# A chain of attention and two feed-forward layers on one core: the pooled values of two head pairs added up by TensorE in PSUM, and a new order of issue

## The chip, the cores and the metric

The kernel runs on one core of a Trainium2 chip. A core has TensorE (PE in the profile; PEld is its loading of weights), VectorE (DVE), ScalarE (ACT), GpSimd (POOL) and SyncE (SP), which here issues every DMA. The metric is the time of one execution on the device in microseconds (us); the profile's span is a little shorter, since it runs from the first to the last instruction.

## The reference

Attention over 4 batches of 8 heads, 576 positions, head size 64; then two feed-forward layers of 2304 tokens, width 512, hidden width 2048. What the change touches is the pooled part of the attention:

```
factor = 4
q_d = q.reshape(B, H, Sd, factor, D).mean(axis=3)      # Sd = 144
k_d = ...;  v_d = v.reshape(B, H, Sd, factor, D).mean(axis=3)
out_d = sm_attn(q_d, k_d, v_d)                         # softmax(q_d k_d^T / 8) v_d
out_up = np.repeat(out_d, factor, axis=2)
... out_local: each position attends to the 3 before and the 3 behind it ...
return out_up + out_local
```

Then `x = moe(x)` with `g = max(h,0) + log1p(exp(-|h|))`, and `moe2(x)` with `g = h * cos(h)`, where `h = x @ w_in` and the result is `g @ w_out`.

## The kernel before

The 32 heads are taken as 16 pairs, p00 to p33 (batch, pair of the batch). The first four, p00 to p03, make the first 512 tokens, from which the first layer starts. A pair goes through steps that the code names by letters. A writes the local scores to PSUM, B the pooled scores (Bm for the first four pairs, Bj inside A for the others). A2, A3, A4, A5, A6 are the local softmax on VectorE and ScalarE, B1, B2, B4 the pooled one. C and D turn the two sets of weights by TensorE (into tiles that ScalarE copies to aT and aTd). E multiplies: `pooled_values` the pooled weights with the pooled values, then 22 matmuls per head with the values themselves (vw, L1199). `up` and E1 add both and write the pair's columns of the tokens (raw0 to raw3 for the first four pairs, one tile each).

The pooled values are made like this before: a tile vd holds the pair's values as 3 blocks of 128 partitions, with the four rows r of a position side by side. `sum3` adds rows 0, 1 to rows 2, 3 (384 results per partition), `sum4` the two that are left (192 results) and writes the tile vs; both are VectorE instructions at L591. `pooled_values` then issues four matmuls: one per head with 128 partitions (L1162), one per head for what is left of the 144 positions (64 partitions, L1167). All are fp32; the profile shows an fp32 matmul as two records.

The first layer (L1 0 f in the code, L1392) needs raw0 to raw3 and the weights w1i, 16 units of 128 columns; six units (f = 0 to 5) are done in fp32, four matmuls each, into two PSUM halves h0 and h1 by turns. Weights come as 64-bit floats, in blocks of 1 MB, into two staging tiles stg0 and stg1, and are made to fp32 by ScalarE (L744, L760) and VectorE (L765, "join2"); a staging tile comes free with its join2. `allmax` (L629, L635) spreads a maximum over the partitions by a small matmul into h, and VectorE reduces it (red).

The order in which each engine issues is fixed before the kernel runs: a planner orders all steps by due times, to which a table MOVES of 739 numbers adds shifts. Each engine then works strictly in that order. Where the planner expects TensorE to stand idle early in the kernel it puts in a filler, a matmul of zeros (L2215, 128x512) whose result nobody reads; fillers are instructions like all others, and stand in the order.

Tiles come in rings: three qk tiles, two vd, three vw, two stg, four double PSUM banks (any0 to any3). A tile's next load waits until its last reader is done, and all loads stand in one order on SP.

Of the kernel before, what the change touches and what calls it, by code (L numbers as in the profile page):

```python
# [24 lines left out]
B, H, S, D = 4, 8, 576, 64  # L25
# [3 lines left out]
SD = S // 4  # L29
# [15 lines left out]
PV = 0  # L45
# [429 lines left out]
def pe(us):  # L475
    return {"pe": us}
# [27 lines left out]
def build(tc, qk, vw, vd, mask, w1i, w1o, w2i, w2o, out):  # L504
    nc = tc.nc
# [1797 lines left out]
```

## Time and profile before

| | |
|---|---|
| time, median of three runs | 828.73 us (827.4 to 828.96) |
| profiled execution: its time, its span | 827.2 us, 825.4 us |
| TensorE busy | 811.2 us, 98% of the span |
| VectorE busy | 736.4 us, 89% |
| ScalarE busy | 524.9 us, 64% |
| HBM read, written | 128.04 MB, 19.40 MB |

Busy time of TensorE includes the 64 fillers, which are no work. So a slice in which TensorE is nine tenths busy can still be one in which it waits; the fillers' own rows tell how much.

### The profile page before, as it was taken

What the parts mean: (1) busy time and instruction counts of PE and PEld (TensorE: products, weight loads), DVE (VectorE), ACT (ScalarE), POOL (GpSimd) and SP (SyncE); (2) the same over time, 40 slices, a digit from 0 to 9 for tenths busy, and PEclk for the clock granted to TensorE, in tenths of its full rate; (3) what the DMA queues carried; (4) which work ended last, traced back from release to release, by engine and by line L of the source; (5) the groups of instructions that cost most, each with busy time, mean ns of one, the idle gap of its engine ahead of it and who ended that gap; (6) DMA issues with size and microseconds to landing.
All of it is one profiled execution on the core that took longest, in us unless ns stands there. A gap on an engine that the chain in (4) does not pass through costs nothing.

```text
span 825.4 us, 17050 instructions
## 1 busy us (share of the span) xinstructions
PE 811.2 (98%) x6970; PEld 554.5 (67%) x6970; DVE 736.4 (89%) x1473; ACT 524.9 (64%) x877; POOL 1.8 (0%) x9
## 2 busy tenths in 40 slices
PE   8989999999999999999999999999999999999997
PEld 3644454555555544444447888888888888888886
DVE  7989989988695679999898999999999999999773
ACT  5887899554233359798997767665645555646420
POOL 0000000000000000000000000000000000000000
PEclk9999999999999999999999999999999999999999
DMA  9987421112200025775674532545666684689574
GB/s 356 348 311 259 162 97 34 41 53 94 80 17 2 1 104 176 233 228 186 235 275 160 216 135 91 178 154 207 231 227 218 222 287 153 251 266 335 183 215 177
DMA packets 49790, 148.54 MB, mean 180 GB/s; under 512 B 3888, under 2 KB 22960, under 8 KB 45616
## 3 DMA queue, kind: packets, MB, share of 16 engines
q1 hardware_dynamic: 49712, 147.46, 51.6%
q8 instruction: 54, 0.88, 0.4%
q14 instruction: 24, 0.20, 0.1%
HBM read 128.04 MB, written 19.40 MB: 179 GB/s over the span
## 4 chain that ended last, share of the span: by engine, by line
PE 79%; ACT 7%; DMA 6%; DVE 6%; issue 1%; POOL 0%; DVEq 0%; ACTq 0%; SPq 0%; POOLq 0%
PE h L1500 20%; PE any L1826 19%; PE any L1724 19%; PE h L1456 16%; DMA stg<-w1i 2%; DMA stg<-w2i 1%; PE any L1199 1%; DMA stg<-w1o 1%; DMA xt<-scr_out 1%; ACT w1i_t L787 1%; PE any L1095 1%; ACT tab L1658 1%; PE any L939 1%; ACT tab L1670 1%; DMA vd<-vd 1%
## 5 line engine op out<-in xcount | busy, mean ns | idle before, releaser
L1456 PE MATMUL h<-xt,w1i_t 128*128 128x512 f16 (+1 forms) x888 | 179.9, 356 | 0.3 <-DVE red L635 0.3
L1724 PE MATMUL any<-g,w1o_t 128*128 128x512 f16 (+1 forms) x792 | 161.6, 353 | 0.2 <-DVE g L599 0.2
L1456 PEld LDWEIGHTS <-w1i_t 128*128 128x128 f16 x888 | 86.0, 98 | 82.9 <-issue 2.9
L1724 PEld LDWEIGHTS <-w1o_t 128*128 128x128 f16 x888 | 85.5, 98 | 79.5 <-issue 2.0
L1500 PEld LDWEIGHTS <-ri 128*128 128x128 f16 x1194 | 116.7, 98 | 13.9 <-DMA ri<-scr_in 0.2
L1826 PEld LDWEIGHTS <-w1i_t 128*128 128x128 f16 x762 | 74.5, 98 | 11.3 <-issue 2.8
L1500 PE MATMUL h<-tx,ri 128*128 128x256 f16 x636 | 81.7, 273 | 0.0
L1826 PEld LDWEIGHTS <-w1o_t 128*128 128x128 f16 x750 | 73.3, 98 | 8.8 <-issue 0.3
L1500 PE MATMUL h<-xt,ri 128*128 128x256 f16 x558 | 74.5, 273 | 0.0
L1826 PE MATMUL any<-ro,w1i_t 128*128 128x256 f16 x489 | 73.0, 273 | 0.9 <-DVE g L1785 0.5
L609 ACT ACTIVATE w1o_t<-gf 128x512 f16<-128x512 f32 (+1 forms) x68 | 39.5, 587 | 52.4 <-DVE gf L591 34.2
L1651 ACT ACTIVATE tab<-h,i 128x512 f32<-128x512 f32 (+1 forms) x64 | 39.6, 631 | 50.7 <-PE h L1456 46.5
L1826 PE MATMUL any<-ro,w1o_t 128*128 128x256 f16 x435 | 66.8, 273 | 0.1
L591 DVE TENSOR_TENSOR hs<-h,hs 128x512 f32<-128x512 f32 (+1 forms) x96 | 56.9, 595 | 0.9 <-PE h L1500 0.4
L609 ACT ACTIVATE w1i_t<-gf 128x256 f16<-128x256 f32 (+2 forms) x82 | 39.8, 506 | 26.1 <-DVE gf L591 13.0
L591 DVE TENSOR_TENSOR gf<-gf 128x256 f32<-128x256 f32 (+2 forms) x120 | 55.1, 471 | 0.2
L1826 PE MATMUL any<-xt,w1o_t 128*128 128x256 f16 x315 | 48.0, 273 | 0.0
L591 DVE TENSOR_TENSOR w1i_t<-gf,w1i_t 128x256 f16<-128x256 f32 (+2 forms) x91 | 46.2, 523 | 0.5 <-ACT w1i_t L609 0.4
L599 DVE SCALAR_TENSOR_TENSOR g<-tab,sg,g 128x512 f16<-128x512 f32 (+1 forms) x64 | 43.2, 680 | 2.6 <-ACT g L603 1.8
L591 DVE TENSOR_TENSOR w1o_t<-gf,w1o_t 128x512 f16<-128x512 f32 (+1 forms) x69 | 43.2, 634 | 0.9 <-ACT w1o_t L609 0.7
L1826 PE MATMUL any<-xt,w1i_t 128*128 128x256 f16 x273 | 42.9, 273 | 1.0 <-ACT g L603 0.4
L1785 DVE SCALAR_TENSOR_TENSOR g<-any,ik,g 128x512 f32<-128x512 f32 (+1 forms) x35 | 23.8, 693 | 18.6 <-PE any L1826 18.5
(236 smaller groups left out, 1376.2 us busy)
## 6 DMA issues: line engine op xcount, KB each, us to landing
ri<-scr_in SPq DMA_DIRECT2D x31, 896.0 KB, 4.8
ro<-scr_out SPq DMA_DIRECT2D x41, 512.0 KB, 4.8
xt<-scr_out SPq DMA_DIRECT2D x29, 512.0 KB, 5.7
qk<-qk SPq DMA_DIRECT2D x16, 589.0 KB, 4.7
stg<-w1i SPq DMA_DIRECT2D x8, 1024.0 KB, 6.7
stg<-w1o SPq DMA_DIRECT2D x8, 1024.0 KB, 5.6
stg<-w2o SPq DMA_DIRECT2D x8, 1024.0 KB, 5.6
stg<-w2i SPq DMA_DIRECT2D x8, 1024.0 KB, 5.7
```

The costliest lines, as they stand in the source:

```text
L591: eng[e].tensor_tensor(out=out, in0=in0, in1=in1, op=op)
L599: nc.vector.scalar_tensor_tensor(out=out, in0=raw, scalar=s, in1=other, op0=ALU.mult, op1=op)
L609: nc.scalar.activation(out=out, in_=in_, func=AF.Copy)
L787: nc.scalar.activation(out=out().rearrange("p (m e) -> p m e", m=2), in_=self.floats(b), func=AF.Abs, accum_out=self.bd[:, b : b + 1],)
L939: nc.tensor.matmul(pa.t[64 * h : 64 * h + 64, j, 64 * g : 64 * g + 64], tk.t[64 * j : 64 * j + 64, 0, q0 + 3 : q0 + 67], tk.t[64 * j : 64 ...
L1095: nc.tensor.transpose(pc.t[:, k, 128 * o : 128 * o + 128], sm.t[:, g, :, :].rearrange("p j k -> p (j k)"), ident)
L1456: nc.tensor.matmul(h.t[:, 0:n], l, r, start=(i == 0), stop=(i == 11))
L1500: nc.tensor.matmul(h.t[:, a : a + m], l, r, start=(i == 0), stop=(i == n - 1))
L1651: act(n, 1, True), lambda: nc.scalar.activation(out=x(), in_=h.t[:, 0:n], func=AF.Softplus, scale=col(o.i1, f)),
L1724: nc.tensor.matmul(a.t[:, i, 0:n], l, r, start=(first and j == 0), stop=(last and j == 2))
L1785: dve(256 * m, False, 1), lambda: nc.vector.scalar_tensor_tensor(out=o.t[:, 0 : 256 * m], in0=view(k), scalar=T[t].ik, in1=x.t[:, 0 : 256 ...
L1826: nc.tensor.matmul(a.t[:, z, 256 * c : 256 * c + 256], l, r, start=(b == 0 and x == 0), stop=(b == NB - 1 and x == 2),)
```

## The change

Where a pair's number is below PV (2 now, 0 before, so p00 and p01), sum3 and sum4 are not issued. `pooled_values` multiplies the pooled weights with each of the four rows of vd instead and lets the four products add up in the same PSUM region: 16 matmuls for the pair in place of 4. The planner's cost of step E for such a pair is set to 3.4 us. The table MOVES is another one, of 798 numbers. Lines behind L85 stand 14 lower in the new file.

```
-PV = 0
+PV = 2
...
-    "L1 0 0 ln#1": -314.5, "L1 0 1 exp#1": 70, "L1 0 1 mm#1": 963, "L1 0 10 G#1": 1002.5, "L1 0 10 abs#1": 29.5,
...
+    "tsum#12": 980.5, "tsum#13": 833, "tsum#15": 852, "tsum#17": 814.9, "tsum#3": 770, "tsum#6": 726, "tsum#7": 728.5,
...
             def pooled_values():
-                for j in range(2):
-                    o = slice(64 * j, 64 * j + 64)
-                    nc.tensor.matmul(
-                        po.t[o, 1 - quads, u0 : u0 + SD], vs.t[:, j, :], aTd.t[:, SD * j : SD * j + SD], start=True, stop=False
-                    )
-                for j in range(2):
-                    o, w = slice(64 * j, 64 * j + 64), left + 16 - 16 * j
-                    nc.tensor.matmul(
-                        po.t[o, 1 - quads, u0 : u0 + SD], vs.t[o, 2, :], aTd.t[o, w : w + SD], start=False, stop=True
-                    )
+                vals = [tv.t[:, :, r, :] for r in range(4)] if i < PV else [vs.t]
+                for z in (False, True):
+                    for n, v in enumerate(vals):
+                        for j in range(2):
+                            o, w = slice(64 * j, 64 * j + 64), left + 16 - 16 * j
+                            l, r = (v[o, 2, :], aTd.t[o, w : w + SD]) if z else (v[:, j, :], aTd.t[:, SD * j : SD * j + SD])
+                            nc.tensor.matmul(
+                                po.t[o, 1 - quads, u0 : u0 + SD], l, r, start=(not z and n == 0),
+                                stop=(z and n == len(vals) - 1),
+                            )
...
-            outs_of.append(aop(pe(3.5 if i < PV else ...
+            outs_of.append(aop(pe(3.4 if i < PV else ...
```

On VectorE, in the first 20 us, the order before was (vd1 and vs1 are p01's; qt, qd are sums of queries and keys; rs the row sums of a softmax; sm and ed its weights; w1i_t the join2 of a weight block):

```order
L591 TENSOR_TENSOR ed0_128<-ed0_128,rs_0_235 128x432
L591 TENSOR_TENSOR qd0_120<-qt0_119 128x288
L591 TENSOR_TENSOR vd1_115<-vd1_115 128x3x128
L978 TENSOR_REDUCE rs_1_236<-sm1_126 128x10
L591 TENSOR_TENSOR vs1_123<-vd1_115 128x192
L981 TENSOR_SCALAR rs_1_236<-rs_1_236 128x13
L965 TENSOR_REDUCE nm_2_233<-any0_87 128x10
L984 RECIPROCAL rs_1_236<-rs_1_236 128x13
L1046 TENSOR_REDUCE nd_2_241<-any1_88 128x3
L591 TENSOR_TENSOR sm1_126<-sm1_126,rs_1_236 128x640
L591 TENSOR_TENSOR ed1_129<-ed1_129,rs_1_236 128x432
L765 SCALAR_TENSOR_TENSOR w1i_t_164<-w1i_t_164,stg1_110 128x1024
```

At the same place, from ed of p00 to the join2 of the second block, it is now:

```order
L605 TENSOR_TENSOR ed0_128<-ed0_128,rs_0_235 128x432
L992 TENSOR_REDUCE rs_1_236<-sm1_126 128x10
L605 TENSOR_TENSOR qt0_119<-qk2_113 128x576
L979 TENSOR_REDUCE nm_2_233<-any0_87 128x10
L605 TENSOR_TENSOR qd0_120<-qt0_119 128x288
L995 TENSOR_SCALAR rs_1_236<-rs_1_236 128x13
L779 SCALAR_TENSOR_TENSOR w1i_t_164<-w1i_t_164,stg0_109 128x1024
L998 RECIPROCAL rs_1_236<-rs_1_236 128x13
L1060 TENSOR_REDUCE nd_2_241<-any3_96 128x3
L605 TENSOR_TENSOR sm1_126<-sm1_126,rs_1_236 128x640
L605 TENSOR_TENSOR ed1_129<-ed1_129,rs_1_236 128x432
L779 SCALAR_TENSOR_TENSOR w1i_t_164<-w1i_t_164,stg1_110 128x1024
```

The two sums of p01 are gone, and the join2 of the first weight block, which stood behind p00's raw0 before, has come ahead of p01's last softmax steps; the sum of p02's queries has moved down to here.

On TensorE step E of p00 (aTd0 and aT0 are the turned weights, zero is a filler) was this before:

```order
L1162 MATMUL any2_92<-aTd0_132,vs0_122 64x144 x2
L1167 MATMUL any2_92<-aTd0_132,vs0_122 64x144 x2
L1199 MATMUL any2_92<-aT0_130,vw0_116 64x58 x16
L1199 MATMUL any2_92<-aT0_130,vw0_116 64x48
L1199 MATMUL any2_92<-aT0_130,vw0_116 64x10
```

And now:

```order
L1180 MATMUL any2_92<-aTd0_132,vd0_114 64x144 x16
L1213 MATMUL any2_92<-aT0_130,vw0_116 64x58 x16
L1213 MATMUL any2_92<-aT0_130,vw0_116 64x48
L1213 MATMUL any2_92<-aT0_130,vw0_116 64x10
L1213 MATMUL any2_92<-aT0_130,vw0_116 64x48
```

Four matmuls on vs have become sixteen on vd, and E reads the tile that the load wrote. Ahead of E of p03, the last of the first four, stand 64 fillers now, where 58 did, and two matmuls of the first layer, where three did; behind it no filler is left, where 6 were.

Further on TensorE, where the first layer's fp32 units run and the tokens' maximum (am0) is spread, the order was, from the end of one unit to the step E of p10 (aTd0, vs1):

```order
L1392 MATMUL h0_627<-raw3_169,w1i_t_164 128x512
L629 LDWEIGHTS am0_243
L629 MATMUL h1_628<-ident_s_74,am0_243 128x128
L1392 MATMUL h1_628<-raw0_166,w1i_t_164 128x512
L1392 MATMUL h1_628<-raw1_167,w1i_t_164 128x512
L1392 MATMUL h1_628<-raw2_168,w1i_t_164 128x512
L1392 MATMUL h1_628<-raw3_169,w1i_t_164 128x512
L1162 MATMUL any2_92<-aTd0_132,vs1_123 64x144 x2
```

It is now, up to the next unit:

```order
L1406 MATMUL h1_691<-raw3_169,w1i_t_164 128x512
L643 LDWEIGHTS am0_243
L643 MATMUL h0_690<-ident_s_74,am0_243 128x128
L1180 MATMUL any0_87<-aTd0_132,vs2_124 64x144 x4
L1213 MATMUL any0_87<-aT0_130,vw1_117 64x58 x14
L1213 MATMUL any0_87<-aT0_130,vw1_117 64x42
L1213 MATMUL any0_87<-aT0_130,vw1_117 64x16
L1213 MATMUL any0_87<-aT0_130,vw1_117 64x42
```

Step E of p10 now stands between the spread of am0 and the next unit that writes the same half of PSUM; before, that unit followed the spread at once.

## Rows read from the trace of the kernel before

**Rows 1.** The page: busy time of each engine, share, instructions.

```profile
PE 811.2 (98%) x6970; PEld 554.5 (67%) x6970; DVE 736.4 (89%) x1473; ACT 524.9 (64%) x877; POOL 1.8 (0%) x9
```

**Rows 2.** Stretches: length, busy us of PE, PEld, DVE, ACT, POOL, clock, DMA.

```profile
0.00:44.57 44.57, 41.25 (x616) 24.11 (x617) 37.95 (x81) 32.11 (x86) 1.77 (x9) 1.00 0.92 352
44.57:69.04 24.47, 20.92 (x113) 9.38 (x110) 22.96 (x50) 21.39 (x38) 0.00 (x0) 1.00 0.78 274
69.04:140.00 70.96, 70.03 (x571) 35.11 (x571) 65.86 (x127) 63.86 (x121) 0.00 (x0) 1.00 0.38 132
140.00:760.00 620.00, 618.87 (x5135) 433.06 (x5134) 568.97 (x1121) 388.32 (x593) 0.00 (x0) 1.00 0.49 167
760.00:825.43 65.43, 60.09 (x544) 52.82 (x541) 40.67 (x101) 19.18 (x42) 0.00 (x0) 1.00 0.61 199
```

**Rows 3.** Line L2215, the fillers: ns shortest/median/longest, first and last start.

```profile
L2215 PE MATMUL any<-zero x56: 376/379/634, 2.1 to 68.7; 128*128 128x512 f16 x56
L2215 PE MATMUL h<-zero x8: 379/379/390, 29.0 to 36.8; 128*128 128x512 f16 x8
```

**Rows 4.** Timeline of PE: start, us, line, tiles, records [idle before, releaser].

```profile
2.06 4.02 PE L2215 MATMUL any<-zero 128*128 128x512 f16 x9 [2.06 <-POOL zero L2204]
...
20.08 0.47 PE L1162 MATMUL any<-aTd,vs 128*64 128x144 f32 x4
20.47 0.46 PE L1167 MATMUL any<-aTd,vs 64*64 64x144 f32 x4
20.77 1.48 PE L1199 MATMUL any<-aT,vw 64*64 64x58 f32 x44
22.18 1.25 PE L2215 MATMUL any<-zero 128*128 128x512 f16 x5
...
29.88 0.71 PE L1095 MATMUL any<-ident,sm 128*128 128x128 f32 x5
...
47.75 2.84 PE L1392 MATMUL h<-raw,w1i_t 128*128 128x512 f32 x6 [1.19 <-DVE raw L1223]
...
56.65 0.22 PE L629 MATMUL h<-ident_s,am 128*128 128x128 bf16 x1 [0.34 <-DVE g L1413]
57.59 3.70 PE L1392 MATMUL h<-raw,w1i_t 128*128 128x512 f32 x8 [0.73 <-DVE red L635]
...
66.67 0.22 PE L629 MATMUL h<-ident_s,bd_w1i 128*128 128x128 bf16 x1 [0.26 <-DVE g L1413]
67.65 0.38 PE L629 MATMUL h<-ident_s,bd_w1i 128*128 128x128 bf16 x4 [0.77 <-DVE red L635]
...
69.04 0.33 PE L933 MATMUL any<-mask_sb,ident_b 64*64 64x320 bf16 x4
```

**Rows 5.** Line L1095: weight loads of the turns, ns shortest/median/longest.

```profile
L1095 PEld LDWEIGHTS any<-ident,sm x80: 137/140/145, 15.3 to 286.5; 128*128 128x128 f32 x80
```

**Rows 6.** Timeline of DVE about the sums of p00 and p01.

```profile
5.63 0.56 DVE L591 TENSOR_TENSOR vd<-vd 128x384 f32<-128x384 f32 x1
6.23 0.36 DVE L591 TENSOR_TENSOR vs<-vd 128x192 f32<-128x192 f32 x1
7.47 0.61 DVE L1046 TENSOR_REDUCE nd<-any 128x3 f32<-128x432 f32 x1 [0.89 <-PE any L1040]
...
16.01 0.57 DVE L591 TENSOR_TENSOR vd<-vd 128x384 f32<-128x384 f32 x1
16.48 0.83 DVE L978 TENSOR_REDUCE rs<-sm 128x10 f32<-128x640 f32 x1
17.20 0.37 DVE L591 TENSOR_TENSOR vs<-vd 128x192 f32<-128x192 f32 x1
```

**Rows 7.** Waits of PE behind 69 us: waiting, releaser, us in total, times, longest.

```profile
PE any L1116 <- ACT ed L1063: 0.6, 1, 0.6
PE h L629 <- ACT stg L1997: 0.5, 1, 0.5
```

**Rows 8.** DMA issues of the values: count, KB each, median us to landing.

```profile
vd<-vd SPq DMA_DIRECT2D x8, 384.0 KB, 5.3
```

More of the change, by code (lines that the diff above doesn't have):

```diff
@@ L1206, in pair @@
             raws += [("x2g", 14 + c // 2)] if b == 2 else []
-            outs_of.append(aop(pe(3.5 if i < PV else 1.38 if small else 1.48 if quads else 2.11), Em, [tv if i < PV else vs, aTd, tw, (aT, 0), (aT, 1)], [po, *outs, *raws], [po, up, aT], nm + "E"))
+            outs_of.append(aop(pe(3.4 if i < PV else 1.38 if small else 1.48 if quads else 2.11), Em, [tv if i < PV else vs, aTd, tw, (aT, 0), (aT, 1)], [po, *outs, *raws], [po, up, aT], nm + "E"))
             if small:
```

296 rows, old and new, of the table MOVES are left out of this document.

## The prediction

> **What bounds the kernel now.** I read the busy shares first [rows 1]: TensorE is busy 98% of the span, every other engine less. Work that is added to TensorE therefore costs its length, unless it takes the place of time in which TensorE does nothing useful, and the stretches [rows 2] tell where that is. From 140 to 760 us TensorE idles 1.1 of 620 us, behind that 5.3 (the last results' way out is most of it). From 0 to 44.57 it idles 3.3, of which 2.06 are the start, from 44.57 to 69.04 3.55, from 69.04 to 140 0.9. The granted clock is 1.00 in all of these, so no term below is one of the clock. Fillers come on top: 64 of them [rows 3], the first nine in 4.02 us, later ones five in some 1.2 [rows 4], all before 69.04. So whatever can be won lies in the first 69 us: there TensorE runs in a row what stands in its order, fillers with it, and its real stops are few. Up to 44.57, the end of E of p03, they sum to 1.26 behind the start; between there and 69.04 the timeline shows one for raw3 (1.19 us) and four in the pattern "a small spread into h, then a wait for VectorE's reduction of it, or for the unit's result that frees h" (0.34, 0.73, 0.26, 0.77) [rows 4].
>
> **The sums that leave VectorE.** Each pair loses two instructions: 0.56 and 0.36 us for p00, 0.57 and 0.37 for p01 [rows 6]. Those of p00 ran while VectorE had nothing else: behind them it still waited 0.89 us for TensorE. They are worth nothing. Those of p01 ran in a full row; successive starts are 0.47 and about 0.27 apart, since neighbours overlap, so VectorE gets 0.74 us there. The new order spends it at once: the first block's join2 comes ahead of p01's last softmax steps, and p01's D is not earlier for it.
>
> **The products that come to TensorE.** Twelve more fp32 matmuls per pair, 24 records, issued by heads in twos that run side by side: 12 steps. The trace has no chain of 16, so I bound a step. Above: the two twos of L1162 take 0.39 us for two steps (20.08 to 20.47), 0.20 a step [rows 4], with the load of the second set of weights in the open. Below: an fp32 record of 512 columns takes (3.70 - 0.59) / 7 = 0.44 us in the unit at 57.59, so 144 columns stream 0.125 us. In long rows of one kind the loads hide: the 22 steps of L1199 take (1.48 - 0.22) / 21 = 0.06 us each at 58 columns, against 0.05 by the same stream, and the five 128-column turns at 29.88 follow each other at (0.71 - 0.27) / 4 = 0.11 us though each load takes 0.14 [rows 4, 5]. Sixteen alike are nearer to these, so I take the lower end: 1.5 us a pair, **3.0 us** in all; with 0.20 it is 4.7. Nothing excuses this time from TensorE's row: it is work, and neither end is below nothing, since no record gets shorter.
> A rule speaks against the change here. The Trainium skill, "TensorE: Matmul & The Clock Gate", section "The mechanism", says that loads of weights overlap with matmuls in flight only when the row group differs, and these sixteen use the same rows. By that rule a step would cost load and stream, 0.13 + 0.125 us, 3.1 us a pair and 6.1 in all in place of 3.0. The turns at 29.88, all 128 rows each time, contradict it here [rows 4, 5]; it stays as a rival below.
>
> **Fillers.** 64 before and after, but eight stand at the start, where nine did; a filler there takes 0.45, later 0.22 to 0.24: -0.2 us. Before E of p03 there are now 64, where 58 were, and one product of the first layer less (0.93). So E of p03 ends later: 44.57 + 3.0 + 1.3 - 0.9 - 0.2 = 47.8. Six fillers fewer stand behind it.
>
> **Stops up to E of p03.** E of p00 waits as before for ScalarE, whose order there still has the first step of the second weight block between two copies of aTd. C of p00 and A of p03 have 0.2 to 0.7 us to wait for. I take +0.1 against the 1.26 of before.
>
> **Stops from there to 69 us.** raw3 stopped TensorE because E of p03 was early and VectorE, in order, came to raw3 late (47.1). Now E ends at 47.8, and VectorE, which at raw3 has two joins more behind it (3.5 us), but not the sums of p00 and p01 nor one pair's sums of queries and keys (2.5; about +1.0 us), comes there at 48 to 49, while TensorE has two products (1.9 us) that don't need it. -1.2. The spread of am0 now has p10's E (1.47 us from its first matmul to the next unit) between it and the next unit of its half, which covers a wait of 0.73; the weights' spreads stand among products of the second matrix, which need no h. -2.1, of which I give back 0.2 for results (g) that may be late. What is late next is VectorE: in this stretch it was busy 23.0 of 24.5 us [rows 2]. Sum -3.1.
>
> **Behind 69 us.** Of the 0.9 idle, 0.6 is D of p11 waiting for ScalarE's ed [rows 7]; a further unit of 2.6 us stands ahead of it now: -0.5. In 140 to 760 the longest stop, 0.5 (with 0.2 behind it) is a spread of weight maxima waiting for ScalarE [rows 7]; in the new order these spreads stand some 30 matmuls of 0.22 us later: -0.7. The last 65 us are ordered anew with as many matmuls and the same last four results; I count 0, with 1.2 us either way.
> The values' tile is now read by E, not by the sums, so the two vd tiles come free later: p02's load goes out behind E of p00 (about 25.7, 6.8 before), and behind it on SP stand p11's queries, p03's vw and the fifth weight block. VectorE needs it at about 29 us, and the load takes 5.3 us in the median [rows 8], but with other loads queued ahead of it; by then the queue is short, so I count nothing for it. If that cover is gone, it is the third rival.
>
> **Sum.** Against the profiled execution, 827.2 us (span 825.4 and 1.8 around it): +3.0 - 0.2 + 0.1 - 3.1 - 0.5 - 0.7 = -1.4, so 825.8. The profiled execution lies 1.5 below the median of the runs shown, 828.73; carried over to that, 827.3 us. The bounds are +1.7 (products at the upper end), 1.2 either way (the tail), and -0.5 to +1 (stops that I gave or kept): own range 825.3 to 829.5. A measurement of this kernel can tell about 0.2%, 1.7 us, from no change.
>
> **Rivals.**
> 1. All stops vanish. If the new order fits as well as it is drawn, the 3.55, 0.9 and 1.1 of idle go whole and of the first 1.26 too: 827.2 + 2.8 - 6.8 = 823.2, 824.7 in the median's terms. For it: nearly all stops lie where the order was redrawn. Against it: VectorE is 94% busy from 44 to 69 us and can't be much earlier. Chance 0.20.
> 2. The change doesn't do what it says: VectorE's 0.74 us buys nothing, stops come back elsewhere, and TensorE pays for its products: 827.2 + 2.8 = 830.0, 831.5. For it: half of what leaves VectorE was hidden. Against: the stops of rows 4 have named causes that the order takes away. Chance 0.08.
> 3. Slower by the values' tile. Place: VectorE's sum of p02, which waits, in order, for a load that goes out only behind E of p00; p03's load hangs on that sum in turn. If the loads take the full 5.3 us, VectorE stands 2 us at each, and p03's softmax, C, E and raw3 with it: 825.8 + 3.9 = 829.7, 831.2. It decides from the point where each of the two waits passes 1.5 us. Against it: TensorE is itself late by then, which takes up the first microsecond. Chance 0.11.
> 4. The loads of the sixteen in the open. A step of 0.255 us, as two records one behind the other with a load between, gives 3.1 us more: 825.8 + 3.1 = 828.9, 830.4 in the median's terms. For it: the two twos of L1162 with 0.20 a step. Against it: the turns with 0.11. Chance 0.05. The rule of the skill named above says just this.
>
> **How the numbers follow.** My forecast has 0.50; 0.23 of it lies below 827.07 (faster by over 0.2%), 0.27 within 0.2%. Rival 1 is faster. Rivals 2 and 3 are slower, of rival 4 half. The remaining 0.06 is spread over lesser mixtures within 0.2%. Faster 0.43, same 0.36, slower 0.21. The range takes in half of rival 1 and most of rival 3: 824.0 to 831.3.
>
> **What would show it.** The new L1180 groups of 16: about 2.2 us from the first to the following L1213 (3.0 would be the upper bound, 3.7 rival 4). E of p03 should end at about 48 us. TensorE should reach the scores of p11 (the row that stood at 69.04) at 68 to 69.5, with less than 0.7 us of stops between; if stops on raw3 or on red stand there as before, the term -3.1 is wrong, and with it the sign. VectorE waiting for vd at p02's or p03's sum shows rival 3. A TensorE that idles more than 1 us from 140 to 760, or more than 6 behind that, would make the last terms wrong.

## The result: slower by one per cent

The changed kernel takes 836.11 us (median of four executions, 834.89 to 838.96) against 828.16 (827.4 to 828.96) for the kernel before, measured beside it: a ratio of 1.0102, with a 95% interval of 1.0078 to 1.0126. The forecast was 827.3, the range ended at 831.3. The profiled execution took 835.9 us, with a span of 834.1, and its span is 8.7 us longer than that of before.

### The profile after

The page of the changed kernel, busy time of each engine, to be held against [rows 1]:

```profile
PE 814.1 (98%) x7018; PEld 557.5 (67%) x7018; DVE 737.0 (88%) x1475; ACT 524.4 (63%) x875; POOL 1.8 (0%) x9
```

TensorE is busy 2.9 us longer; VectorE and ScalarE are within 0.6 us of where they were. So 5.8 of the 8.7 us are time in which TensorE does nothing. The stretches say where; they end at the same steps as those of [rows 2] (the end of E of p03, the scores of p11, 140, 760, the end). Columns: length, then busy us and records of PE, PEld, DVE, ACT, POOL, the granted clock, DMA.

```profile
0.00:51.42 51.42, 44.01 (x668) 27.15 (x668) 39.84 (x80) 34.32 (x84) 1.77 (x9) 1.00 0.86 323
51.42:72.22 20.80, 19.55 (x104) 8.86 (x101) 18.70 (x41) 18.23 (x39) 0.00 (x0) 1.00 0.86 313
72.22:140.00 67.78, 64.99 (x498) 31.80 (x498) 59.01 (x118) 56.27 (x110) 0.00 (x0) 1.00 0.37 126
140.00:760.00 620.00, 616.31 (x5127) 428.64 (x5127) 569.13 (x1122) 389.23 (x596) 0.00 (x0) 1.00 0.48 162
760.00:834.05 74.05, 69.20 (x628) 61.00 (x625) 50.30 (x118) 26.40 (x52) 0.00 (x0) 1.00 0.68 221
```

Length less busy time of PE, before and after: 3.3 and 7.4 up to the end of E of p03, 3.6 and 1.3 from there to the scores of p11, 0.9 and 2.8 from there to 140, 1.1 and 3.7 from 140 to 760, 5.3 and 4.9 behind. The stops between E of p03 and the scores of p11 did go, as the prediction said. New ones came ahead of that stretch and behind it. The scores of p11 begin at 72.22 in place of 69.04, 3.2 us late, and 5.5 us more are lost behind them (4.0 of them idle time of TensorE, 1.5 longer busy time), where the prediction had put nothing but small gains.

The timeline of PE shows what was foreseen (start, us, line, tiles, records, and in brackets the idle time before and what ended it):

```profile
22.32 2.33 PE L1180 MATMUL any<-aTd,vd 128*64 128x144 f32 x32
24.48 1.48 PE L1213 MATMUL any<-aT,vw 64*64 64x58 f32 x44
...
40.90 0.74 PE L1109 MATMUL any<-ident,sm 128*128 128x128 f32 x5 [2.23 <-DVE sm L605]
...
50.01 1.48 PE L1213 MATMUL any<-aT,vw 64*64 64x58 f32 x44
51.42 2.03 PE L1406 MATMUL h<-raw,w1i_t 128*128 128x512 f32 x4
53.90 1.98 PE L1406 MATMUL h<-raw,w1i_t 128*128 128x512 f32 x4 [0.44 <-DVE raw L1237]
...
63.53 0.22 PE L643 MATMUL h<-ident_s,am 128*128 128x128 bf16 x1 [0.17 <-DVE g L1427]
...
65.16 7.13 PE L1406 MATMUL h<-raw,w1i_t 128*128 128x512 f32 x16
72.22 0.33 PE L947 MATMUL any<-mask_sb,ident_b 64*64 64x320 bf16 x4
```

The 32 records of p00's pooled values take 24.48 - 22.32 = 2.16 us, where 0.69 stood [rows 4]. The stop at raw3 is 0.44 us in place of 1.19, that at the spread of x's maxima 0.17 in place of 0.34, and the four units at 65.16 run through. But C of p03 stops TensorE for 2.23 us at 38.67, and what it waits for is VectorE. VectorE's timeline ahead of that:

```profile
31.75 0.56 DVE L605 TENSOR_TENSOR vd<-vd 128x384 f32<-128x384 f32 x1 [1.90 <-DMA vd<-vd]
...
38.73 0.56 DVE L605 TENSOR_TENSOR vd<-vd 128x384 f32<-128x384 f32 x1 [0.96 <-DMA vd<-vd]
...
45.30 0.56 DVE L605 TENSOR_TENSOR vd<-vd 128x384 f32<-128x384 f32 x1 [1.90 <-DMA vd<-vd]
```

These are the sums over the values of p02, p03 and p10, each waiting for its load: the third rival of the prediction. Behind the scores of p11 the stops are spread; the longest four in the timeline of PE:

```profile
92.45 0.22 PE L643 MATMUL h<-ident_s,bd_w1o 128*128 128x128 bf16 x1 [2.06 <-DVE g L1427]
...
142.16 0.59 PE L1130 MATMUL any<-ident,ed 128*128 128x128 f32 x3 [0.62 <-DVE s_w1i L602]
...
180.26 0.76 PE L1109 MATMUL any<-ident,sm 128*128 128x128 f32 x5 [0.73 <-DVE sm L605]
...
241.29 0.47 PE L1188 MATMUL any<-aTd,vs 64*64 64x144 f32 x8 [0.71 <-ACT aT L623]
```

Two explanations offer themselves. HOLD: the tiles of p00's and p01's values are held until E, so later values load late, VectorE falls behind in the front and everything pays for that. ORDER: the order that was fitted anew, on all engines and for the whole kernel, is itself the worse one.

### The profile page after: what moved, and what is told of

Read it like the earlier page. It is cut to its first block, busy times and chain, and to the rows that moved or that the text cites. A ratio compares the mean times of both kernels' runs of the same rounds, so it can differ in the third digit from the quotient of the medians.

```text
span 834.1 us, 17153 instructions
## 1 busy us (share of the span) xinstructions
PE 814.1 (98%) x7018; PEld 557.5 (67%) x7018; DVE 737.0 (88%) x1475; ACT 524.4 (63%) x875; POOL 1.8 (0%) x9
## 4 chain that ended last, share of the span: by engine, by line
PE 65%; DVE 14%; DMA 9%; ACT 9%; issue 2%; SPq 1%; POOL 0%; DVEq 0%; POOLq 0%; ACTq 0%
PE h L1514 18%; PE any L1840 18%; PE any L1738 14%; PE h L1470 10%; DMA vd<-vd 3%; DMA stg<-w1o 2%; DMA stg<-w1i 2%; DMA stg<-w2o 1%; DVE sm L605 1%; DMA scr_out<-dec 1%; ACT ed L1077 1%; DMA stg<-w2i 1%; PE any L1213 1%; DVE hs L605 1%; DVE gf L605 1%
## 5 line engine op out<-in xcount | busy, mean ns | idle before, releaser
L1738 PEld LDWEIGHTS <-w1o_t 128*128 128x128 f16 x888 | 85.4, 98 | 78.9 <-issue 2.0
L1514 PEld LDWEIGHTS <-ri 128*128 128x128 f16 x1086 | 106.2, 98 | 12.6
L1840 PE MATMUL any<-ro,w1i_t 128*128 128x256 f16 x543 | 80.7, 273 | 0.4 <-ACT g L617 0.4
L1840 PEld LDWEIGHTS <-w1o_t 128*128 128x128 f16 x732 | 71.5, 98 | 9.4 <-issue 1.1
L1514 PE MATMUL h<-tx,ri 128*128 128x256 f16 x582 | 74.5, 273 | 0.0
L1514 PE MATMUL h<-xt,ri 128*128 128x256 f16 x504 | 67.1, 273 | 0.0
L1840 PE MATMUL any<-ro,w1o_t 128*128 128x256 f16 x417 | 63.7, 273 | 0.2 <-DVE g L1799 0.2
L623 ACT ACTIVATE w1o_t<-gf 128x512 f16<-128x512 f32 (+1 forms) x64 | 37.3, 590 | 39.0 <-DVE gf L605 30.9
L605 DVE TENSOR_TENSOR w1i_t<-gf,w1i_t 128x256 f16<-128x256 f32 (+2 forms) x93 | 47.8, 531 | 0.0
L1514 PEld LDWEIGHTS <-xt 128*128 128x128 f16 x450 | 44.0, 98 | 5.3 <-issue 0.3
```

The source lines that it names most:

```text
L605: eng[e].tensor_tensor(out=out, in0=in0, in1=in1, op=op)
L623: nc.scalar.activation(out=out, in_=in_, func=AF.Copy)
L1514: nc.tensor.matmul(h.t[:, a : a + m], l, r, start=(i == 0), stop=(i == n - 1))
L1738: nc.tensor.matmul(a.t[:, i, 0:n], l, r, start=(first and j == 0), stop=(last and j == 2))
L1840: nc.tensor.matmul(a.t[:, z, 256 * c : 256 * c + 256], l, r, start=(b == 0 and x == 0), stop=(b == NB - 1 and x == 2),)
```

## Experiments

All times are medians of 4 to 12 executions; the ratio is to the kernel before, run on the same chip beside it.

| run | us | ratio, 95% interval |
|---|---|---|
| vd4 | 834.12 | 1.0070, 1.0055 to 1.0086 |
| vd4_early | 834.85 | 1.0081, 1.0063 to 1.0099 |
| b_vd4 | 828.40 | 1.0003, 0.9990 to 1.0016 |
| b_own | 828.54 | 1.0013, 1.0001 to 1.0026 |
| h_own_p11 | 834.73 | 1.0087, 1.0068 to 1.0106 |
| h_after_p11 | 832.76 | 1.0070, 1.0044 to 1.0095 |
| h_own_p30 | 835.84 | 1.0101, 1.0080 to 1.0122 |
| h_after_p30 | 838.48 | 1.0128, 1.0102 to 1.0153 |
| eased | 836.94 | 1.0120, 1.0081 to 1.0158 |
| b_eased | 829.78 | 1.0026, 1.0012 to 1.0040 |
| vd4_light | 833.04 | 1.0053, 1.0026 to 1.0079 |
| own_light | 828.73 | 1.0014, 1.0002 to 1.0027 |
| order_alone | 836.72 | 1.0108, 1.0087 to 1.0130 |
| own_again | 828.90 | 1.0011, 0.9996 to 1.0027 |

### The tiles: vd4, vd4_early, b_vd4

The order of issue is planned as it was, and only then the first eight pairs' values are handed out to four tiles in place of two; the two new ones lie in the space of x's fourth tile.

```diff
+VDX, VDP = 4, 8
...
 ops, all4 = P.order(), list(BANK.tiles)
+for c in range(VDX - NVD):
+    VD.tiles.append(xt[3][:, 2 * c : 2 * c + 2].rearrange("p c (a r d) -> p (c a) r d", r=4, d=64))
...
+for m, v in enumerate(sorted(use, key=lambda v: use[v][0])):
+    v.i = min(range(VDX if m < VDP else NVD), key=lambda k: over[k])
+    assert over[v.i] < use[v][0]
+    over[v.i] = use[v][-1]
```

vd4 does this to the changed kernel, b_vd4 to the kernel before. vd4_early besides puts two loads forward in SyncE's row:

```diff
+MOVED = [('p02 vd#1', 'p02 vw#1'), ('p03 vd#1', 'p10 qk#1')]
```

> The changed kernel, order of issue on every engine untouched, but the first eight pairs' values have four tiles vd in place of two (two views of x's fourth tile, which nothing writes before the third batch entry). The load of p02's values then no longer waits for E of p00, and p03's not for the sums of p02. Theory HOLD (the loss of some 8 us is the tiles held until E, through VectorE's waits of 1.9, 0.96, 1.9 and 0.2 us for these loads): most of those 5.0 us comes back, and the stop of TensorE at C of p03 (2.2 us) with it: 831 to 833 us, ratio to the kernel before 1.003 to 1.006. Theory ORDER (the order fitted anew asks for things later or earlier than they are there, whatever the tiles): SyncE issues these loads behind other transfers and VectorE waits for other things instead: 834.5 to 836.5, ratio 1.008 to 1.010.

> As the run with four tiles vd, and the loads of the values of p02 and p03 moved forward in SyncE's row: p02's ahead of the load of its windows, p03's ahead of p10's queries, as early as the kernel before has them. Theory HOLD: VectorE's waits for values are gone to under 0.3 us in the first 40 us, and the time is at most that of four tiles alone, 830 to 833. Theory ORDER: what was wanted early now takes bandwidth from weights and queries, and VectorE waits for those: no gain over four tiles alone (within 0.5 us), or a loss of up to 1 us.

> The kernel before, order untouched, with the four tiles vd for the first eight pairs: the control for the runs with four tiles. SyncE there waited 9.4 us for the sums vs and 6.8 for a load vd before it could load values; VectorE never waited for values. HOLD and ORDER agree: the tiles are not short there, so 827.5 to 829, ratio 0.998 to 1.001.

VectorE's waits for loads in vd4, behind 27 us:

```profile
30.72 0.56 DVE L606 TENSOR_TENSOR xt<-xt 128x384 f32<-128x384 f32 x1 [0.84 <-DMA xt<-vd]
...
37.17 0.56 DVE L606 TENSOR_TENSOR xt<-xt 128x384 f32<-128x384 f32 x1 [0.44 <-DMA xt<-vd]
...
44.05 0.56 DVE L606 TENSOR_TENSOR vd<-vd 128x384 f32<-128x384 f32 x1 [2.21 <-DMA vd<-vd]
```

The waits of p02 and p03 shrink from 1.90 and 0.96 to 0.84 and 0.44, that of p10 stays. (xt is the borrowed space.) TensorE's stop at C of p03 falls from 2.23 to 0.69 us, but a new one of 1.02 us stands at 68.17, so the scores of p11 come only 0.4 us earlier, at 71.81. The time falls by 2.0 us to 834.1, between what the two expected and nearer to ORDER's 834.5 than to HOLD's 831 to 833; the interval overlaps a little with that of the changed kernel. In vd4_early the loads of p02 and p03 go out at 8.0 and 19.4 us, and VectorE waits for neither, as HOLD had asked; the time is 0.7 us longer all the same. So the held tile is real and worth about 2 of the 8 us (1.3 by the two profiled spans, 834.1 and 832.8); the other 6 are elsewhere. In the order of before the tiles are not short: b_vd4 is not to be told from before.

### The change alone: b_own

```diff
+PVE = 2
...
 def sum3():
+    if i < PVE:
+        return
...
+vals = [tv.t[:, :, r, :] for r in range(4)] if i < PVE else [vs.t]
```

The order of before on every engine; p00 and p01 emit no sums (sum3, sum4) and sixteen matmuls.

> The kernel before in its own order of issue, with the change alone: p00 and p01 emit no sums of their values on VectorE, and their E multiplies the four rows in PSUM (four tiles vd, so that nothing waits for a tile). It is the change without the refitted order and without the held tiles. HOLD: 24 more steps of TensorE (1.5 us a pair) and nothing else: 830 to 831.5, ratio 1.003 to 1.004. ORDER expects the same or better, since VectorE has 1.7 us less to do in the first 30 us: 828.5 to 831. A time of 833 or more would say that the sum in PSUM costs more than its steps, and would refute both.

Stretches of b_own, up to its scores of p11, 140, 760 and the end:

```profile
0.00:71.04 71.04, 64.69 (x774) 36.64 (x774) 59.84 (x125) 53.92 (x123) 1.77 (x9) 1.00 0.85 315
71.04:140.00 68.96, 67.90 (x537) 33.89 (x540) 63.73 (x124) 61.73 (x118) 0.00 (x0) 1.00 0.38 134
140.00:760.00 620.00, 619.43 (x5170) 433.54 (x5162) 569.65 (x1121) 389.70 (x594) 0.00 (x0) 1.00 0.49 167
760.00:826.00 66.00, 61.09 (x554) 53.91 (x552) 41.82 (x103) 20.01 (x43) 0.00 (x0) 1.00 0.62 202
```

828.54 us, 0.95 above the kernel before: what ORDER expected (828.5 to 831), and below HOLD's 830. TensorE has its 24 more steps, and the scores of p11 come 2.0 us later than in [rows 4]; from 140 to 760 it idles 0.6 us, where the changed kernel idles 3.7. The sums in PSUM by themselves cost next to nothing. With four tiles in both, the refitted order is 5.6 us slower than the order of before (834.12 and 828.54). HOLD is refuted as the main cause.

### Where in the order: four kernels put together

Each takes the one order up to a step (the seam) and the other for what is left; computation and four tiles as in vd4 and b_own. At the scores of p11 the two orders have done nearly the same work: by its records TensorE lacks there, in the refitted order, only the five spreads of w1i's maxima (0.6 us in [rows 4]).

```diff
-ops, all4 = P.order(), list(BANK.tiles)
+ops, all4 = P.replay(), list(BANK.tiles)
```

replay issues operations in the order of a list, and hands out tiles as they come free in that list.

> Both orders of issue with the changed computation and four tiles vd; they have done nearly the same work when TensorE comes to the scores of p11 (71.0 us in the order of before, 71.8 in the refitted one). Here the order of before up to there, the refitted one for all that is left. Whole orders: 828.5 (order of before) and 834.1 (refitted). Theory LAG (the refitted front leaves VectorE late, and the stops behind 72 us pay for it): with the other front they go, 828.5 to 830.5. Theory PLACE (the refitted order behind the front is itself too tight): 832.5 to 834.

> The converse: the refitted order up to the scores of p11, then the order of before for what is left. LAG: 832.5 to 834.5. PLACE: only the front's own 0.8 us is lost, 828.8 to 830.5.

> The order of before up to the scores of p30 (225 us in both), the refitted one behind. By the two traces 2 us of the difference lies behind this point. LAG: nothing of it is left, 828 to 829.5. PLACE: 829.8 to 831.5.

> The refitted order up to the scores of p30, then the order of before. LAG: the late stops stay as long as the refitted order lasts and nothing heals them: 832.5 to 834.5. PLACE: 0.8 of the front and some 3.8 from there to p30 are lost, 2 are won back: 831.5 to 833.

Two stretches, up to the scores of p11 and behind them, of h_own_p11 and then of h_after_p11:

```profile
0.00:72.47 72.47, 65.13 (x775) 36.71 (x775) 61.71 (x128) 53.86 (x123) 1.77 (x9) 0.99 0.85 316
72.47:833.20 760.73, 750.14 (x6245) 521.94 (x6244) 675.93 (x1349) 470.42 (x751) 0.00 (x0) 1.00 0.48 165
```

```profile
0.00:74.44 74.44, 64.55 (x774) 37.27 (x774) 62.17 (x127) 55.70 (x125) 1.77 (x9) 0.99 0.86 325
74.44:830.40 755.96, 750.02 (x6245) 522.88 (x6244) 673.71 (x1341) 470.43 (x753) 0.00 (x0) 1.00 0.48 165
```

The refitted order behind the scores of p11 takes 760.7 us although the front ahead of it is that of before; the order of before takes 756.0 behind the refitted front. Both stretches have the same 6245 records of TensorE, so no work of TensorE that slipped over the seam makes the difference. This is PLACE, not LAG, though 834.7 lies a little above PLACE's 834. The stops are even the same ones, here in h_own_p11, beside those of the changed kernel above:

```profile
141.26 0.58 PE L1251 MATMUL any<-ident,ed 128*128 128x128 f32 x3 [0.62 <-DVE s_w1i L723]
...
179.36 0.77 PE L1230 MATMUL any<-ident,sm 128*128 128x128 f32 x5 [0.72 <-DVE sm L726]
...
240.38 0.48 PE L1309 MATMUL any<-aTd,vs 64*64 64x144 f32 x8 [0.71 <-ACT aT L744]
```

The whole time of h_after_p11, 832.8, is above what PLACE expected (828.8 to 830.5): its front ends at 74.44, 2.6 us later than that of vd4, with one stop of 2.3 us just at the seam. About that stop the granted clock was low as well, 0.57 from 72 to 80 us, which is some 3.4 us (an estimate: 0.43 of 8). The two runs with the seam at p30 are above both theories, 835.8 and 838.5. At p30 the orders have done different work, and TensorE stops 4.1 and 2.8 us there in the two traces. They show nothing but that a seam can cost.

### Can the stops be moved away: eased, b_eased

Steps of TensorE that stop it are put one or two places later in its row, so that matmuls that stand ready go first. The kernel holds the finished row; these are the moves, step and places:

```
("wmax spread#4", 2), ("p12 E#1", 1), ("p13 D#1", 1), ("p20 D#1", 2), ("p20 C#1", 1),
("p21 D#1", 1), ("p23 E#1", 1), ("p33 A#1", 1)
```

b_eased does it in the kernel before, with L1 0 4 mm#1, wmax spread#1, p11 D#1, L1 0 14 mm#1, p33 A#1 and wmax spread#8, one place each. By the traces two steps of VectorE in eased and one in b_eased also changed places with a neighbour.

> The refitted order with four tiles vd, and eight of TensorE's steps behind 72 us put one or two steps later in its row, on no other engine anything: the spread of the maxima of w1o that stopped 1.79 us at 91.3, E of p12 (0.28 at 119.5), D of p13 (0.62 at 140.9), C and D of p20 (0.73 at 179.0), D of p21 (0.34 at 191.7), E of p23 (0.71 at 240.0), the scores of p33 (0.36 at 278.4). 4.8 us of stops in sum, of 834.1 us. Theory TIGHT (the refitted order asks TensorE for these steps a fraction of a microsecond before VectorE or ScalarE has their inputs, while other matmuls stand ready behind): the stops go and nothing takes their place, 829.5 to 831. Theory BOUND (VectorE is the limit of these stretches, TensorE only waits for it there): stops come back behind, 833 to 834.5.

> The kernel before, its own computation and tiles, with six steps of TensorE put one place later in its row: the first of the unit that waits 0.73 us for the maxima of x at 57.6 goes behind E of p10, the spread that waits 0.77 at 67.7 behind the scores of p11, D of p11 (0.62 at 86.5), the unit at 124.5 (0.30), the scores of p33 (0.31), the spread of w2's maxima (0.54 at 405). 3.3 us of stops in sum. TIGHT: 1.5 to 3 us less than before, 824.5 to 826.5. BOUND: within 0.7 us of before, since what comes from VectorE is late however the row stands.

TIGHT fell, in both. Stops came back, as BOUND has it, but both times lie above its ranges too (836.9 against 834.5, 829.8 against 828.3). Of the stops named for eased none is left where it was, but new ones stand beside them; behind 72 us the stops over 0.15 us sum to 8.8 us in eased, 7.3 in vd4. Behind the scores of p11 eased takes 763.0 us, vd4 761.0. Four of the stops of eased:

```profile
89.79 1.98 PE L1564 MATMUL any<-g,w1o_t 128*128 128x512 f32 x4 [1.16 <-DVE g L1548]
99.13 0.61 PE L1251 MATMUL any<-ident,ed 128*128 128x128 f32 x3 [1.56 <-ACT aT L744]
...
137.51 1.04 PE L1859 MATMUL any<-g,w1o_t 128*128 128x512 f16 x4 [0.68 <-DVE w1o_t L734]
...
187.92 1.46 PE L1591 MATMUL h<-xt,w1i_t 128*128 128x512 f16 x6 [0.98 <-ACT ed L1198]
```

The first is plainest: the spread at 91.3 waited for VectorE's result g, since that frees the half of PSUM; with the spread out of the way the next product waits for the same g. The spread itself comes later, and VectorE waits 1.81 us for its result:

```profile
94.46 0.29 DVE L770 TENSOR_REDUCE red<-h 128x1 f32<-128x128 f32 x1 [1.81 <-PE h L764]
```

b_eased shows that the order of before is no different: six moves meant to win 3.3 us made it 2.2 us slower (829.78 against 827.59; some 0.4 of that may be the issue from a list, by own_again below), with a stop of 1.43 us at the first spread of w1i in place of 0.26:

```profile
67.53 0.22 PE L751 MATMUL h<-ident_s,bd_w1i 128*128 128x128 bf16 x1 [1.43 <-DVE g L1535]
```

### Less work for VectorE: vd4_light, own_light

```diff
-two("dve", q, x[:, :, :, 0:2], x[:, :, :, 2:4], ALU.add)
+n = 1 if i >= 5 else 2
+two("dve", q[:, 0:n], x[:, 0:n, :, 0:2], x[:, 0:n, :, 2:4], ALU.add)
...
-x = tv.t[:, 0:nv]
+x = tv.t[:, 0 : 1 if i >= 5 else nv]
```

> The refitted order with four tiles vd, no step moved, but VectorE has less to do from p11 on: the sums over queries (sum1) take one of the two halves and the sums over values (sum3, sum4) one of four parts, so that some 1.1 us a pair for 11 pairs, 12 us between about 50 and 300 us, is left out (the pooled queries and values of these pairs are therefore not all summed). Theory BOUND (behind 72 us the refitted order leaves TensorE waiting because VectorE's work there is late): of 7.3 us of stops behind 72 us more than half go, 829.5 to 831.5 us against 834.1. Theory ORDER (what TensorE waits for is set by the position of the steps in each row, not by VectorE's load): 833 to 835, and the stops keep their places.

> The same work left out from VectorE in the order of before with the change alone (828.5 us, 2.8 us of stops behind 72 us): the control. BOUND: at most 1.5 us less, 827 to 828.5, and the distance between the two orders falls from 5.6 us to under 3.5. ORDER: 827.5 to 829, and the distance stays 4.5 to 6.5.

834.1 became 833.0, 828.5 became 828.7: each time is in ORDER's range, but the distance between the orders is 4.3 us in place of 5.6, between the two theories, and the executions of vd4_light spread from 830.8 to 835.5. The same stops of TensorE are there, shorter; in vd4_light:

```profile
91.92 0.22 PE L644 MATMUL h<-ident_s,bd_w1o 128*128 128x128 bf16 x1 [0.88 <-DVE g L1430]
...
141.17 0.58 PE L1133 MATMUL any<-ident,ed 128*128 128x128 f32 x3 [0.42 <-DVE s_w1i L603]
...
239.35 0.47 PE L1191 MATMUL any<-aTd,vs 64*64 64x144 f32 x8 [0.42 <-ACT aT L624]
```

1.79, 0.62 and 0.71 of vd4 became 0.88, 0.42 and 0.42. In this profiled execution the front ended 2.0 us later than that of vd4, with a granted clock of 0.95 (below), so the stretch behind the scores of p11 says it better: 832.7 - 73.8 = 758.9 us, against 761.0 in vd4, while own_light with 755.2 is where b_own was (755.0). VectorE's busy time fell by 8.0 us (736.6 to 728.6), not by the 12 that were expected. So 8 us less for VectorE take about 2 us from a distance of 6, in one execution each: VectorE's load is a part of it, and the rest I put down to the places of the steps.

### The order alone: order_alone, own_again

order_alone has the computation of before in the refitted order: the sums of p00 and p01 are back on VectorE (sum3 right behind A5, sum4 right behind A6 of the same pair), their E has one operand, all else stands where the refitted order has it. own_again is b_own once more, issued from a list as the kernels put together are.

> The refitted order alone: the computation of before (the values of p00 and p01 summed on VectorE, right behind the sums and the scaling of their weights, and E of the two with one operand), every other step where the refitted order has it, four tiles vd. ORDER (the loss is the refitted order's, whatever is computed): 834.1 less the 2.9 us of the 24 steps, 830.5 to 832.5 us, against 828.4 of the order of before with the same computation and tiles. Theory JOINT (the order is only bad with the sums in PSUM, whose long E keeps TensorE and the tiles): 828 to 829.5.

> A control for the runs that are put together from two orders: the order of before with the change alone once more, every row on every engine as in that run, but handed out from a list, with other numbers of tiles among equals. Whatever it differs from 828.5 is what the putting together costs: under 1 us if the seams are to be trusted to that, else the runs at p30 say nothing.

order_alone takes 836.72 us, 8.3 more than b_vd4, which does the same with the same tiles. JOINT is refuted, and ORDER did not expect as much. Part of the excess may be the clock: in the profiled execution it was 0.95 up to 74 us and 0.996 over the whole, some 3.3 us (an estimate: 0.004 of 834), and the mean was 0.993 to 0.998 in all four executions, where vd4 had 0.999 or 1.0. Stretches of order_alone, and its stops behind:

```profile
0.00:74.00 74.00, 63.82 (x721) 35.20 (x721) 60.48 (x125) 53.03 (x122) 1.77 (x9) 0.95 0.86 313
74.00:834.40 760.40, 749.42 (x6250) 521.49 (x6249) 678.06 (x1355) 471.25 (x753) 0.00 (x0) 1.00 0.48 165
```

```profile
143.20 0.58 PE L1238 MATMUL any<-ident,ed 128*128 128x128 f32 x3 [0.62 <-DVE s_w1i L710]
...
181.30 0.77 PE L1217 MATMUL any<-ident,sm 128*128 128x128 f32 x5 [0.72 <-DVE sm L713]
...
242.32 0.48 PE L1296 MATMUL any<-aTd,vs 64*64 64x144 f32 x8 [0.71 <-ACT aT L731]
```

0.62, 0.72 and 0.71 again, at the same steps, with no sum in PSUM anywhere. own_again is 828.9, 0.4 us more than b_own, so issuing from a list costs little. The spans behind the scores of p11 make the verdict plain:

| behind the scores of p11 | us |
|---|---|
| order of before: before, b_own, h_after_p11, own_again | 756.4, 755.0, 756.0, 756.5 |
| refitted order: after, vd4, h_own_p11, order_alone | 761.9, 761.0, 760.7, 760.4 |

Two fronts, two counts of tiles and two computations are in these rows, and only the order of what is issued behind tells them apart: 5.0 us between the means. That vd4 is 2.6 us faster than order_alone is less than that clock may have cost, so it says nothing on the sums in PSUM.

What is called an order here holds one thing more: the planner also chooses the engine of steps that either VectorE or ScalarE can do. The changed kernel's VectorE has four sums less, but is busy 0.6 us longer, and ScalarE loads the tables of its functions 39 times, 35 before. The four more loads stand between 300 and 760 us, where TensorE has one stop over 0.15 us (0.52). No run parts the two in the refitted order, so "order" stands for both.

## Why the prediction was wrong

**The products, the fillers.** Right. (What the four sums are worth on VectorE was not measured apart; b_own, 0.1 us above b_vd4, has their going and the products together.) The groups take 2.16 us, 2.2 were forecast, 3.0 and 3.7 are refuted, and with them rival 4. TensorE's busy time grew by 2.9, +3.0 was the term. The number of fillers stayed at 64. That these sixteen "use the same rows" holds for the first eight; the other eight take the lower and the upper 64 rows in turn.

**Stops up to E of p03, +0.1.** The first wrong step. Idle time up to that end grew by 4.1 us (3.3 to 7.4), and E of p03 ended at 51.4 in place of 47.8. I had gone through the stops of before and asked what becomes of each; the new order made stops that have no row in [rows 4], above all the 2.23 us at C of p03, and two of 1.3 us together for loads of queries.

**The values' tile, "by then the queue is short, so I count nothing for it".** Wrong in the same place: the loads land 6.8 us after issue in the median, 5.3 before [rows 8], and VectorE waits 1.90, 0.96 and 1.90 us for three of them. The mechanism was the third rival's, which had 0.11 and a price of 3.9 us; by vd4 it is worth about 2.0. p10's wait is not the tile's: it stays with four tiles (2.21 us).

**Stops from there to 69 us, -3.1.** Right in kind, a bit large: idle time there fell from 3.55 to 1.25, by 2.3, and the stops went for the named reasons. Some gain of this kind needs no refit: with the order of before TensorE idles 12.9 us of b_own's span of 826.0, against 15.2 of b_vd4's 825.5 and 14.3 of before, in one execution each.

**Behind 69 us, -0.5 and -0.7.** The largest wrong step: 5.1 us of the 10 between the forecast of -1.4 and the 8.7 of the span; the stops up to E of p03 are 4.0. The two stops that were to go did go: D of p11, at 100.0 us now, and the spread of 405 us have none. But up to 760 us TensorE idles 4.4 us more behind the scores of p11, at steps that did not stop it before. The prediction read the change there as a matter of which of the old stops go, and gave the tail 1.2 us either way. It said itself that more than 1 us of idle time from 140 to 760 would make these terms wrong; it is 3.7.

**Rival 2** ("the change doesn't do what it says") had 0.08 and 831.5. Its sum allowed for no loss from the order either. The case that happened, an order that is worse by itself ahead of 51 us and behind 72, was none of the rivals. It should have been the first: the diff replaces the whole table that sets the order, and behind 69 us TensorE idled 2.0 us in 690 up to 760, so there was little to win there and much to lose.

**What stays open.** What makes this order the worse one is not settled. It is no single stop: moving eight of them brought others. VectorE's load is about 2 of the 5 to 6 us. Whether the rest is the sequence or the choice of engines is not shown; exchanging the row of a single engine between the orders was not tried. No kernel here beats the kernel before.

## What to carry to other kernels

When a change comes with an order that was fitted anew, judge the two apart: here the change costs 0 to 1 us in the old order, and the new order 5.6 (vd4 against b_own). An order in which the bounding engine idles 0.3% of a stretch has little to win there: six and eight moves that were meant to help cost some 2 us each here, and the refit some 5. For an order that is so full, one of the rivals should have the refit lose. Of tiles that a change holds longer, follow the load that waits for them through its queue to the instruction that stands for it in order.

## What the runs showed of the hardware

The sixteen fp32 matmuls of a pair, 144 columns each, in twos side by side and two records each, follow each other at 2.16 / 16 = 0.135 us a step. A load of their weights takes 0.133 us itself, and the first eight matmuls, all on 128 rows, take 1.14 us (22.31 to 23.45), 0.14 a step:

```profile
L1180 PEld LDWEIGHTS any<-aTd,vd x64: 129/133/137, 22.3 to 34.5; 128*64 128x64 f32 x32, 64*64 64x64 f32 x32
```

```profile
22.31 0.93 PEld L1180 LDWEIGHTS any<-aTd,vd 128*64 128x64 f32 x16 [0.42 <-issue]
23.45 0.93 PEld L1180 LDWEIGHTS any<-aTd,vd 64*64 64x64 f32 x16 [0.20 <-issue]
```

The Trainium skill, "TensorE: Matmul & The Clock Gate", section "The mechanism", lists that loads overlap with matmuls in flight only where the row group differs, though its text above the list also names a background weight buffer as a way. By the list a step would be some 0.26, an estimate from a load of 0.133 and columns of 0.125. The measurement decides: the loads are hidden in a row of this kind too.

The clock can fall after one stop in the front. In vd4_light TensorE stopped 1.82 us for a load of queries, and the granted clock went to 0.50, the 1.2 GHz level, behind it; columns as above:

```profile
15.57 0.71 PE L956 MATMUL any<-qk 64*64 64x64 f32 x24 [1.82 <-DMA qk<-qk]
```

```profile
10.00:14.60 4.60, 3.27 (x66) 1.48 (x55) 4.57 (x10) 2.40 (x5) 0.00 (x0) 1.00 1.01 408
...
16.00:18.00 2.00, 2.00 (x34) 1.73 (x27) 1.94 (x6) 0.25 (x2) 0.00 (x0) 0.50 0.95 391
18.00:20.00 2.00, 2.00 (x11) 1.01 (x9) 1.31 (x3) 0.77 (x2) 0.00 (x0) 0.68 0.47 185
```

In vd4 the same load stopped it 0.74 us, and the clock stayed at 1.00; the scores of p03 came 2.5 us earlier there (20.23 and 22.74): 1.1 of that is the shorter stop, which leaves 1.4 for the clock. In eased and order_alone the same load stopped TensorE 1.85 and 2.24 us, and the clock was 0.50 behind it too. In h_after_p11 it stopped 2.32 us and the clock stayed at 1.00, as it did behind the changed kernel's 2.23 us at 38.67. What tells these apart, no run here shows.
